# Three buffers for a batch's rows, transposes spread over two pairs, stacking in a new order, loads issued four and eight steps later

## The chip, the cores and the metric

One NeuronCore of a Trainium2 chip runs the whole program as one launch. The metric is the device time of one execution in microseconds; the time before is the median of three runs. TensorE is the matrix engine, VectorE, ScalarE and GpSimd are the three others, SyncE only issues transfers here; the profile writes them PE, DVE, ACT, POOL and SP.

## The reference

Attention with a threshold on the scores, for 8 batches of 8 heads, 576 tokens and 64 features a head, then a layer of 8 experts with one expert per token:

```python
scores = scale * np.matmul(q, k.transpose(0, 1, 3, 2))
thresh = np.max(scores, axis=-1, keepdims=True) - tau
scores = np.where(scores >= thresh, scores, -1000000000.0)
attn = np.exp(scores - np.max(scores, axis=-1, keepdims=True))
x = (attn / (attn.sum(-1, keepdims=True) + 1e-09)) @ v      # heads side by side: rows of 512
logits = x @ w_gate
expert_idx = np.argmax(logits, axis=1)
for e in range(E):                                        # 8 experts, 512 -> 1024 -> 512
    mask = expert_idx == e
    ye = np.maximum(x[mask] @ w1[e], 0.0) @ w2[e]
    out[mask] = gate_w[mask, None] * ye                   # gate_w: softmax weight of the chosen expert
```

## The kernel before

**Pairs and steps.** The attention part works on 32 pairs of heads, four to a batch, each in ten steps; step k belongs to pair k // 10. In one step PE computes one tile of transposed scores of that pair (`st_unit`: the `st` matmuls of L455 and L389, two products because queries and keys are held as a high and a low half in float16), ACT takes its exponential (L485 or L469), and DVE multiplies it with the mask "score not under the threshold" (L488, L470). In the same step PE computes one tile of plain scores of the pair two further on (`s_unit`: L405 and L408), and DVE reduces it to row maxima (L418). The maxima of a pair are turned by PE (`pst`, L429), split into three float16 rows (`ptT`) and sent by DMA into three extra rows of the buffer `CQ` of that pair, so that the next pair's `st` product already has the threshold subtracted. Between them stand the pieces of the product with the values of the pair before (`av_piece`, L534 to L546), nine to a pair, one to a step, from the step that `av` in the table `TUNE` names.

**What feeds a pair.** `load_qk` and `load_v` fetch queries, keys and values by DMAs issued from ACT's queue. `split` makes the high and low halves `hi` and `lo` (ACT L302 and L304, then POOL). `stack` copies them by twelve DMAs into the layout that PE wants: per head `QK` and `ck` (four DMAs, functions `first` and `low`) and the queries once more into `CQ` (`query`, two per head). All of these are issued from SP's queue, except that for the pairs 10, 14, 18, 22, 26 and 30 (`crowded`) the queries are issued from ACT's queue, two and three steps later. `split_v` casts the values to float16 in `vop`.

**Batch ends.** After each batch's last pair, `finish` normalizes its rows `R` (four tiles of 128 tokens, and a fifth half-tile `Rh` for every second batch) and SP issues one DMA transpose for each (`turn`, L627), 14 to 16 steps after; `logits`, `route`, `ranks` and the indirect sends (`send`, POOL L725) of the rows to the expert buffers in DRAM follow in the steps of the next pairs. `R` has two buffers; the numbers of the rows (`ids`, L688 and L690) are copied into them by ACT, which must wait until the sends of the batch before have read the buffer.

**What sets the order.** `plan` and `after(k, f, where)` put closures into numbered steps, in front, in the middle or at the end of one, and that order is each engine's program order, up to the end of the attention part (step 320, less 16). The experts after it are ordered by the framework's scheduler. Every engine works through its queue in order. The framework adds semaphore waits by itself; the DMAs of SP and ACT together take eight completion counters in turn, and a DMA waits until the one that had its counter before has landed.

Of the kernel before, what the change touches and what calls it, by code (L numbers as in the profile page):

```python
# [10 lines left out]
F16 = mybir.dt.float16  # L11
F32 = mybir.dt.float32
I32 = mybir.dt.int32
# [31 lines left out]
CAP = NTOK  # L45

TUNE = dict(
    lead=10, cast=1, sl=10, ll=15, sp0=6, sps=0, lv=-9, sv=-2, av=2, tr=4, d=2, lg=5, d5=2, d6=2, d7=1, lg7=9, km=16, rate=15, dh=1, do=3, w1d=5, plv=1, xv=3, so=0, sto=0, ord=0, sc=5, fa=3, fd=4, wa1=-70, wa2=-86, wl1=-28, wl2=-6, avb=2, route=1, ranks=7, pp=8, ew=4, maskat=0, w1a=-40, w1b=3,
)


# [1 line left out]
def kernel(  # L53
# [36 lines left out]

    NM = 3
    KC = 64 + NM
    NB = 3
    NQ = 4
    NV = NT
    cks = [[cpool.tile([P, S], F16, name=f"ck_{i}_{a}") for a in range(2)] for i in range(NQ)]
    cqs = [op.tile([P, 9 * P], F16, tag=f"CQ{i}", name=f"CQ_{i}", bufs=1) for i in range(NQ)]
    vops = [cpool.tile([P, NV, 2 * D + 1], F16, name=f"vop_{i}") for i in range(NB)]
    vfs = [cpool.tile([P, 10, D + 1], F32, name=f"vf_{i}") for i in range(NB)]

    def fill(i, eng):
        for a in range(2):
# [148 lines left out]
    def after(k, f, where=END):  # L251
        plan(now[0] + k, f, where)
# [54 lines left out]
    def stack(n):  # L307
        d = st[n]
        hi, lo = d["hi"], d["lo"]
        d["CK"] = cks[n % NQ]  # L310
        d["QA"], d["KB"] = [], []

        d["CQ"] = CQ = cqs[n % NQ]
        if n >= NQ:
            nc.gpsimd.memset(CQ[64:KC].bitcast(U32), 0)
        def first(a, QK, r):
            return [
                lambda e: e.dma_start(QK[0:64], hi[r]),
                lambda e: e.dma_start(QK[64:128, 1], hi[r, 1]),
            ]  # L320
# [12 lines left out]

        heads = []
        for a in range(2):
            QK = op.tile([P, 2, S], F16, tag=f"QK{a}", name=f"QK_{n}_{a}")
            heads.append((a, QK, slice(64 * a, 64 * a + 64)))
            d["QA"].append(QK[:, 0])
            d["KB"].append(QK[:, 1])
        x, y = heads  # L340
        if n == 1:
            for h, e in ((x, nc.sync), (y, nc.scalar)):
                for f in first(*h) + query(*h) + low(*h):
                    f(e)
            return
        if n == 2:
            for part in first, query, low:
                for h in heads:
                    for f in part(*h):
                        f(nc.sync)  # L350
            return
        for h in heads:
            (f0, f1), (l0, l1) = first(*h), low(*h)
            for f in f0, l0, f1, l1:
                f(nc.sync)
        crowded = n > 9 and n % 4 == 2
        for i, f in enumerate(f for h in heads for f in query(*h)):
            if crowded:
                after(2 + i // 2, lambda f=f: f(nc.scalar))
            else:  # L360
                f(nc.sync)

    def split_v(n):
        vop, x = vops[n % NB], vfs[n % NB][:, 0:NV, 0:D]
# [55 lines left out]
    def parts(n):  # L420


        nm = st[n]["nm"]
        r = small.tile([P, 9], F32, tag="r", name=f"r_{n}")
        nc.vector.tensor_reduce(r, nm.rearrange("p a t -> p t a"), axis=AX.X, op=ALU.min)

        def turn():
            ps = ps_m.tile([P, 512], F32, tag="m", name=f"pst_{n}")
            nc.tensor.transpose(ps[0:9, 0:P], r, ident)  # L429
            x, y = ps[0:9, 0:P], ps[0:9, P:2 * P]  # L430
            t = small.tile([9, 3, P], F16, tag="ptT", name=f"ptT_{n}", bufs=1)
            v, a = nc.vector, nc.scalar
            for i, f in enumerate((
                lambda: (a.activation(t[:, 0], x, AF.Identity, bias=thr[0:9]), n or rows(t, 0)),
                lambda: v.scalar_tensor_tensor(y, x, thr[0:9], t[:, 0], ALU.add, ALU.subtract),
                lambda: (a.copy(t[:, 1], y), n or rows(t, 1)),
                lambda: (v.tensor_tensor(t[:, 2], y, t[:, 1], ALU.subtract), rows(t, *(range(3) if n else (2,)))),
            )):
                after(i, f, MID)

        def rows(t, *ps):
            for p in ps:
                (nc.sync if n else nc.scalar).dma_start(
                    st[n]["CQ"][64 + p:65 + p].rearrange("p (t c) -> p t c", t=9), t[:, p]
                )

        after(3 if n else 1, turn, FRONT)

    def st_unit(n, t):
# [10 lines left out]
        if t in WHOLE:  # L460
            if t == CORNER:
                pf = pp.tile([P, w], F32, tag="pfc", name=f"e_{n}_{t}", bufs=2)
            elif "pe" in d:
                pf = d.pop("pe")[:, 1]
            else:
                d["pe"] = pp.tile([P, 2, 512], F32, tag="pf", name=f"e_{n}_{t}", bufs=5)
                pf = d["pe"][:, 0]
            d["Pf"][t] = pf
            nc.scalar.activation(pf, sc, AF.Exp, bias=ntau_f, scale=0.125 / SS)  # L469
            return lambda: nc.vector.scalar_tensor_tensor(pf, sc, 0.0, pf, ALU.is_ge, ALU.mult)  # L470
# [25 lines left out]
        return mask  # L496


    sent = set()
    sends = []  # L500
    SYNC = mybir.DependencyInfo(mybir.DependencyClass.Sync, mybir.DependencyReason.DATA)
    W = D + 1
    Rs = [rpool.tile([P, NT, ROW], I32, name=f"R_{i}") for i in range(2)]
    Rh = [rpool.tile([P, ROW], I32, name=f"Rh_{i}") for i in range(2)]
    xhs = [rpool.tile([P, H, W], F32, name=f"xh_{i}") for i in range(2)]

    def row(b, j):
        return Rs[b % 2][:, j] if j < NT else Rh[b // 2 % 2]

    def halves(x):  # L510
        return x.bitcast(F16).rearrange("p (c h d) -> p c h d", c=4, h=2)
# [76 lines left out]
            finish(b)  # L588

    def rounded(b, hp, x, js, eng):  # L590
        o = Rs[b % 2][:, js, 0:DM].bitcast(F16).rearrange("p j (c h d) -> p j c h d", c=4, h=2)[:, :, hp]
        x = x[:, js].rearrange("p j u d -> p j (u d)")

        def low():
            eng.tensor_tensor(o[:, :, 1], x, o[:, :, 0], ALU.subtract)

        def high():
            nc.scalar.copy(o[:, :, 0], x)
            after(1, low)

        after(int(eng is nc.gpsimd), high)

    def finish(b):
# [19 lines left out]
        def turn(j):  # L623
            if j % 2 == 0:
                xTs["t"] = rpool.tile([P, 2, 8, P], F16, tag="xT", name=f"xTg_{b}_{j}", bufs=3)
            xTs[j] = xT = xTs["t"][:, j % 2]
            nc.sync.dma_start_transpose(xT, row(b, j)[:, 0:DM].bitcast(F16))  # L627

        if n > NT:
            after(1 if last else 2, lone)  # L630
        t0 = 2 if last else 14 if b < B - 2 else 7
        for j in range(n):
            after(t0 + (j // 2 if t0 == 14 else j), lambda j=j: turn(j))
        d = t0 + ((n - 1) // 2 if t0 == 14 else n - 1)
# [24 lines left out]
    def route(b, n, dist, Lj, w, got):  # L659
# [25 lines left out]

        def ids(b, n):
            t = tid[:, b // 2]
            nc.scalar.copy(Rs[b % 2][:, :, DM + 1:DM + 2], t[:, 4 * (b % 2):4 * (b % 2) + NT].unsqueeze(2))  # L688
            if n > NT:
                nc.scalar.copy(row(b, NT)[:, DM + 1:DM + 2], t[:, 8:9])  # L690

        def gate(b, n):
            c = 1.0 / (SX * SW * SW)
            nc.scalar.activation(Rs[b % 2].bitcast(F32)[:, :, DM:DM + 1], sm[:, 0:NT], AF.Copy, scale=c)
            if n > NT:
                nc.scalar.activation(row(b, NT).bitcast(F32)[:, DM:DM + 1], sm[:, NT], AF.Copy, scale=c)

        def ranks():
# [239 lines left out]
    def fetch(m):  # L938
# [3 lines left out]
        if m in range(NF, NF + 2):  # L942

            Rm = row(B - 2, m - NF)
            at = 4 * ROW - (2 - (m - NF)) * DM
            xT = Rs[B % 2].rearrange("p j c -> p (j c)")[:, at:at + DM].bitcast(F16)
# [473 lines left out]
```

## Time and profile before

| what | before |
|---|---|
| median of 3 runs (977.92 to 983.87) | 979.29 us |
| the profiled execution | 990.7 us |
| its span, first to last instruction | 989.0 us |
| mean granted clock of TensorE | 0.972 |
| busy time of PE, DVE, ACT, POOL | 899.4, 643.1, 588.5, 496.5 us |
| the attention part within the span | to about 540 us |

The profile shows one execution. Its own time is 1.7 us above its span, and 11.4 us above the median of the runs. The granted clock is the share of TensorE's full speed (2.4 GHz) that the chip allowed in a stretch, so 0.50 is 1.2 GHz.

### The profile page before, as it was taken

How to read it: one execution, taken by the hardware profiler on the slowest of the kernel's cores; microseconds unless marked ns; L12 is line 12 of the kernel's file. 1: busy time of each engine (PE TensorE's matmuls, PEld its weight loads, DVE VectorE, ACT ScalarE, POOL GpSimd, SP SyncE). 2: the span in 40 equal slices, each digit the busy share in tenths (PEclk: the TensorE clock that was granted, in tenths of full speed). 3: DMA queues.
4: the chain of work that ended last, by engine and by line, in shares of the span. 5: the costliest groups of instructions: out<-in, count | busy, mean ns of one | idle time of the engine just before them, and what ended most of it. 6: DMA issues, size and time to landing. Idle time of an engine off the chain costs nothing. (4 is left out here: it accounts for less than half of the span.)

```text
span 989.0 us, 34524 instructions
## 1 busy us (share of the span) xinstructions
PE 899.4 (91%) x14655; PEld 647.8 (66%) x14655; DVE 643.1 (65%) x1322; ACT 588.5 (60%) x1042; POOL 496.5 (50%) x478
## 2 busy tenths in 40 slices
PE   4899988989989799899887797899999999999996
PEld 2477766757767577667665674777766677666773
DVE  7999969868878679697796845825342433424551
ACT  4799877958778587778665732524342433424551
POOL 7577756957858668578656422531222122212121
PEclk9999999989989999999998899999999999999999
DMA  7645575675845946646547549897556746558740
GB/s 190 157 120 142 120 150 125 160 136 140 180 100 137 182 107 167 148 111 163 111 108 143 152 152 314 246 257 233 174 156 165 243 113 207 159 153 189 233 145 25
DMA packets 178301, 158.55 MB, mean 160 GB/s; under 512 B 134557, under 2 KB 150431, under 8 KB 178144
## 3 DMA queue, kind: packets, MB, share of 16 engines
q1 hardware_dynamic: 123642, 98.86, 41.2%
q10 hardware_dynamic: 45510, 28.28, 10.9%
q0 software_dynamic: 8992, 29.18, 8.9%
q8 instruction: 116, 1.90, 0.8%
q14 instruction: 41, 0.34, 0.1%
HBM read 90.56 MB, written 19.17 MB: 111 GB/s over the span
## 5 line engine op out<-in xcount | busy, mean ns | idle before, releaser
L418 DVE TENSOR_REDUCE nm<-s 128x1 f32<-128x512 f32 (+1 forms) x320 | 200.3, 634 | 7.6 <-PE s L408 6.1
L389 PEld LDWEIGHTS <-wb 128*128 128x128 f16 x2304 | 186.9, 100 | 24.4 <-issue 5.1
L389 PE MATMUL y<-wb,hl 128*128 128x512 f16 (+2 forms) x1104 | 196.2, 347 | 0.0
L389 PE MATMUL h<-xTm,wb 128*128 128x256 f16 (+3 forms) x2112 | 191.6, 252 | 1.3 <-DVE e L470 0.7
L455 PE MATMUL st<-QK 128*64 128x64 f16 (+1 forms) x1152 | 147.2, 297 | 30.9 <-DVE e L488 20.2
L494 POOL TENSOR_TENSOR pl<-e,ph 128x1024 f16<-128x1024 f32 x63 | 135.0, 2144 | 78.8 <-ACT ph L493 70.4
L470 DVE SCALAR_TENSOR_TENSOR e<-st,e 128x512 f32<-128x512 f32 (+1 forms) x224 | 134.8, 614 | 49.5 <-ACT e L469 49.5
L405 PE MATMUL s<-QK 128*64 128x64 f16 (+1 forms) x1152 | 145.8, 296 | 20.8 <-POOL QK L135 8.2
L930 DVE SCALAR_TENSOR_TENSOR wb<-wf,wb 128x1024 f16<-128x1024 f32 x96 | 117.3, 1257 | 62.0 <-ACT wb L929 60.0
L389 PEld LDWEIGHTS <-hl 128*128 128x128 f16 (+2 forms) x1104 | 89.0, 98 | 97.6 <-issue 1.3
L408 PE MATMUL s<-ck,CQ 128*64 128x64 f16 (+1 forms) x1152 | 146.4, 294 | 1.5 <-DMA ck<-lo 1.5
L389 PE MATMUL st<-CQ,ck 128*64 128x64 f16 (+1 forms) x1152 | 142.2, 295 | 0.7 <-DMA CQ<-ptT 0.5
L469 ACT ACTIVATE e<-st,ntau_f 128x512 f32<-128x512 f32 (+1 forms) x224 | 133.5, 624 | 15.3 <-PE st L389 12.4
L485 ACT ACTIVATE e<-st,ntau 128x512 f32<-128x512 f32 x128 | 87.7, 685 | 58.7 <-PE st L389 24.5
L1068 POOL DMA_INDIRECT out_dram<-o,gt x39 | 43.2, 1107 | 156.1 <-ACT o L1065 144.9
L929 ACT ACTIVATE wb<-wf 128x1024 f16<-128x1024 f32 x96 | 97.5, 1050 | 35.2 <-DMA wf<-in_w_dram 15.5
L1016 ACT ACTIVATE hl<-h 128x512 f16<-128x512 f32 (+2 forms) x78 | 44.6, 572 | 120.1 <-PE h L389 102.5
L405 PEld LDWEIGHTS <-QK 128*64 128x64 f16 x1152 | 68.0, 115 | 61.4 <-issue 24.7
L488 DVE SCALAR_TENSOR_TENSOR e<-st,e 128x512 f32<-128x512 f32 x128 | 85.9, 672 | 24.9 <-ACT e L485 24.1
L455 PEld LDWEIGHTS <-QK 128*64 128x64 f16 x1152 | 64.9, 114 | 43.8 <-issue 35.2
L537 PE MATMUL av<-vf,e 128*64 128x65 f32 x2048 | 86.8, 225 | 0.7 <-issue 0.7
L537 PEld LDWEIGHTS av<-vf,e 128*64 128x64 f32 x2048 | 82.7, 142 | 1.2 <-issue 0.9
(228 smaller groups left out, 1453.0 us busy)
## 6 DMA issues: line engine op xcount, KB each, us to landing
wf<-in_w_dram SPq DMA_DIRECT2D x96, 512.0 KB
qkf<-in_qk_dram ACTq DMA_DIRECT2D x29, 576.0 KB
vf<-in_v_dram ACTq DMA_DIRECT2D x30, 320.0 KB
QK<-hi SPq DMA_DIRECT2D x61, 144.0 KB
QK<-hi SPq DMA_DIRECT2D x61, 72.0 KB
QK<-lo SPq DMA_DIRECT2D x61, 72.0 KB
ck<-lo SPq DMA_DIRECT2D x61, 72.0 KB
CQ<-hi SPq DMA_DIRECT2D x49, 64.0 KB
```

What stands on the lines that cost most here:

```text
L389: x = nc.tensor.matmul(*a, **kw).ins
L405: nc.tensor.matmul(sc[rows, oc], d["QA"][a][:, cols], d["KB"][a][:, CH[c]], start=True, stop=False)
L408: nc.tensor.matmul(sc[rows, oc], d["CQ"][:, at:at + cols.stop - cols.start], d["CK"][a][:, CH[c]], start=False, stop=True,)
L418: nc.vector.tensor_reduce(o, sc[:, 0:width(t)], axis=AX.X, op=ALU.max, negate=True)
L455: nc.tensor.matmul(sc[rows, oc], d["KB"][a][:, cols], d["QA"][a][:, CH[c]], start=True, stop=False)
L469: nc.scalar.activation(pf, sc, AF.Exp, bias=ntau_f, scale=0.125 / SS)
L470: return lambda: nc.vector.scalar_tensor_tensor(pf, sc, 0.0, pf, ALU.is_ge, ALU.mult)
L485: nc.scalar.activation(pf, sc, AF.Exp, bias=ntau, scale=0.125 / SS)
L494: (nc.vector if (n, t) in PLV else nc.gpsimd).tensor_tensor(l, pd, h, ALU.subtract)
L537: mm(av[rows, 1], pf[NT + j][:, q], vf[:, NT + j], start=False, stop=False)
L929: nc.scalar.activation(o[:, :, 0], x, AF.Copy, scale=SW)
L930: nc.vector.scalar_tensor_tensor(o[:, :, 1], x, SW, o[:, :, 0], ALU.mult, ALU.subtract)
```

## The change

A third buffer for the rows `R` (and one less for `vop`, `vf`, and one less of five for the float32 exponentials `pf`, to make room). The transposes of a batch's rows go to 16, 17, 18, 26 and 27 steps after its end instead of 14, 14, 15, 15, 16, and `logits` and all that follows it ten steps later; the last two batches stay as they were, and the sixth has its own list. The stacking of every pair is issued from SP, in the order `first`, `query`, `low`. `load_qk` moves from 5 to 9 within its pair's steps (`ll`), `load_v` from step 1 to step 9 (`lv`), `split_v` from step 8 of the pair before to step 4 (`sv`), `av` starts at step 1 instead of 2, and the three `rows` DMAs go out one step later. Before each indirect send POOL writes one element to a tile of its own (`apart`).

```diff
-    lead=10, ... ll=15, sp0=6, sps=0, lv=-9, sv=-2, av=2, ...
+    lead=10, ... ll=11, sp0=6, sps=0, lv=-1, sv=4, av=1, ...
...
-    NB = 3
+    NB = 2
...
-        for h in heads:
-            (f0, f1), (l0, l1) = first(*h), low(*h)
-            for f in f0, l0, f1, l1:
-                f(nc.sync)
-        crowded = n > 9 and n % 4 == 2
-        for i, f in enumerate(f for h in heads for f in query(*h)):
-            if crowded:
-                after(2 + i // 2, lambda f=f: f(nc.scalar))
-            else:
-                f(nc.sync)
+        for part in first, query, low:
+            for h in heads:
+                for f in part(*h):
+                    f(nc.sync)
...
-                lambda: (v.tensor_tensor(t[:, 2], y, t[:, 1], ALU.subtract), rows(t, *(range(3) if n else (2,)))),
+                lambda: (v.tensor_tensor(t[:, 2], y, t[:, 1], ALU.subtract), n or rows(t, 2)),
+                lambda: n and rows(t, *range(3)),
...
-                d["pe"] = pp.tile([P, 2, 512], F32, tag="pf", name=f"e_{n}_{t}", bufs=5)
+                d["pe"] = pp.tile([P, 2, 512], F32, tag="pf", name=f"e_{n}_{t}")
...
+    apart = small.tile([1, 1], F32, tag="apart", name="apart", bufs=1)
-    Rs = [rpool.tile([P, NT, ROW], I32, name=f"R_{i}") for i in range(2)]
+    NR = 3
+    Rs = [rpool.tile([P, NT, ROW], I32, name=f"R_{i}") for i in range(NR)]
...
-        t0 = 2 if last else 14 if b < B - 2 else 7
+        turns = {B - 1: range(2, 7), B - 2: range(7, 12), B - 3: (16, 16, 17, 17, 18)}.get(b, (16, 17, 18, 26, 27))
         for j in range(n):
-            after(t0 + (j // 2 if t0 == 14 else j), lambda j=j: turn(j))
-        d = t0 + ((n - 1) // 2 if t0 == 14 else n - 1)
+            after(turns[j], lambda j=j: turn(j))
+        d = turns[n - 1]
...
             def send(j):
+                nc.gpsimd.memset(apart, 0.0)
                 dma = nc.gpsimd.indirect_dma_start(
```

Three places of the program show the new order. In the rows below a name such as `CQ_2` is a buffer, `QK_10_0` the first head of pair 10, `e_7_2` the exponential of pair 7's tile 2.

SP's queue where the first batch's rows are transposed (pair 7), before and then after:

```order
119 L443 DMA CQ_3_107<-ptT_7_2889 1x9x128 x3
120 L627 DMA_TRANSPOSE xTg_0_0_3064<-R_0_197 128x8x128 x2
121 L627 DMA_TRANSPOSE xTg_0_2_3095<-R_0_197 128x8x128 x2
122 L318 DMA QK_10_0_3250<-hi_10_2976 64x1152
123 L324 DMA QK_10_0_3250<-lo_10_2977 64x576
124 L319 DMA QK_10_0_3250<-hi_10_2976 64x576
125 L325 DMA ck_2_0_100<-lo_10_2977 64x576
126 L318 DMA QK_10_1_3251<-hi_10_2976 64x1152
```

```order
119 L432 DMA CQ_3_107<-ptT_7_2890 1x9x128 x3
120 L618 DMA_TRANSPOSE xTg_0_0_3094<-R_0_196 128x8x128 x2
121 L618 DMA_TRANSPOSE xTg_0_2_3173<-R_0_196 128x8x128
122 L318 DMA QK_10_0_3266<-hi_10_2979 64x1152
123 L319 DMA QK_10_0_3266<-hi_10_2979 64x576
124 L318 DMA QK_10_1_3267<-hi_10_2979 64x1152
125 L319 DMA QK_10_1_3267<-hi_10_2979 64x576
126 L330 DMA CQ_2_106<-hi_10_2979 64x512
127 L331 DMA CQ_2_106<-hi_10_2979 64x64
128 L330 DMA CQ_2_106<-hi_10_2979 64x512
129 L331 DMA CQ_2_106<-hi_10_2979 64x64
130 L324 DMA QK_10_0_3266<-lo_10_2980 64x576
```

Four transposes stood in a row ahead of the stacking of pair 10; now three do, the fourth comes a pair later, and the queries (`CQ_2`) stand in SP's queue ahead of the `lo` halves.

ACT's queue in the same pair 7, before and then after:

```order
204 L434 ACTIVATE ptT_8_3304<-pst_8_3302,thr_155 9x128
205 L330 DMA CQ_2_106<-hi_10_2976 64x512
206 L331 DMA CQ_2_106<-hi_10_2976 64x64
207 L485 ACTIVATE e_7_2_3311<-st_7_3_3337,ntau_157 128x512
208 L330 DMA CQ_2_106<-hi_10_2976 64x512
209 L331 DMA CQ_2_106<-hi_10_2976 64x64
210 L493 CAST ph_7_0_3239<-e_7_0_3238 128x1024
```

```order
202 L422 ACTIVATE ptT_8_3308<-pst_8_3306,thr_153 9x128
203 L474 ACTIVATE e_7_2_3315<-st_7_3_3338,ntau_155 128x512
204 L482 CAST ph_7_0_3255<-e_7_0_3254 128x1024
205 L458 ACTIVATE e_7_8_3370<-st_7_8_3365,ntau_f_156 128x512
```

The four DMAs of the queries, between which an exponential stood, are gone from ACT.

ACT's queue in a pair without a batch end (pair 5), before and then after:

```order
157 L469 ACTIVATE e_5_8_2539<-st_5_8_2534,ntau_f_158 128x512
158 L469 ACTIVATE e_5_10_2546<-st_5_10_2541,ntau_f_158 128x64
159 L436 CAST ptT_6_2476<-pst_6_2474 9x128
160 L302 ACTIVATE qkf_9_2236<-qkf_9_2236 128x1152
161 L469 ACTIVATE e_5_8_2539<-st_5_9_2577,ntau_f_158 128x512
162 L288 DMA qkf_10_2649<-in_qk_dram 128x1152
163 L493 CAST ph_5_2_2484<-e_5_2_2483 128x1024
164 L304 CAST hi_9_2563<-qkf_9_2236 128x1152
165 L598 CAST R_0_197<-xn_3_2399 128x4x128
166 L469 ACTIVATE e_5_4_2671<-st_5_4_2666,ntau_f_158 128x512
```

```order
155 L458 ACTIVATE e_5_8_2539<-st_5_8_2534,ntau_f_156 128x512
156 L458 ACTIVATE e_5_10_2546<-st_5_10_2541,ntau_f_156 128x64
157 L424 CAST ptT_6_2477<-pst_6_2475 9x128
158 L353 ACTIVATE vop_1_109<-vf_1_111 128x4x64
159 L302 ACTIVATE qkf_9_2388<-qkf_9_2388 128x1152
160 L589 CAST R_0_196<-xn_3_2371 128x4x128
161 L458 ACTIVATE e_5_8_2539<-st_5_9_2580,ntau_f_156 128x512
162 L482 CAST ph_5_2_2485<-e_5_2_2484 128x1024
163 L304 CAST hi_9_2566<-qkf_9_2388 128x1152
164 L458 ACTIVATE e_5_4_2670<-st_5_4_2665,ntau_f_156 128x512
```

The cast of the values (`vop`) now stands ahead of the split of pair 9 (`qkf_9`), the cast of the rows `R` moved up behind it, and the load of `qkf_10` left this place.

## Rows read from the trace of the kernel before

**Rows 1.** The page, part 1: busy us, share of the span, instructions.

```profile
PE 899.4 (91%) x14655; PEld 647.8 (66%) x14655; DVE 643.1 (65%) x1322; ACT 588.5 (60%) x1042; POOL 496.5 (50%) x478
```

**Rows 2.** Waits of PE, 120 to 540 us: us in total, times, longest.

```profile
PE st L455 <- DVE e L488: 18.8, 6, 5.4
...
PE st L455 <- DVE e L470: 4.8, 9, 1.3
PE s L405 <- DVE e L470: 3.4, 3, 1.3
PE s L405 <- DVE nm L418: 2.9, 10, 0.3
PE pst L429 <- DVE row L748: 2.4, 1, 2.4
```

**Rows 3.** Waits of ACT, 120 to 540 us.

```profile
ACT e L485 <- DMA CQ<-hi: 16.8, 3, 5.9
...
ACT e L485 <- DMA QK<-hi: 7.5, 1, 7.5
ACT e L485 <- DMA QK<-lo: 5.2, 1, 5.2
ACT R L688 <- issue: 4.5, 1, 4.5
ACT Rh L690 <- DMA xs<-Rh,posi: 3.2, 1, 3.2
```

**Rows 4.** SP's timeline at the first batch end: start us, us, operation, count.

```profile
126.44 6.00 SPq L627 DMA_TRANSPOSE xTg<-R  x4
```

**Rows 5.** ACT's timeline there; brackets: idle before, and what ended it.

```profile
138.68 0.69 ACT L485 ACTIVATE e<-st,ntau 128x512 f32<-128x512 f32 x1 [5.18 <-DMA QK<-lo]
```

**Rows 6.** PE's timeline there.

```profile
140.14 0.22 PE L455 MATMUL st<-QK 128*64 128x64 f16 x2 [3.05 <-DVE e L488]
```

**Rows 7.** Windows: us, busy of PE, PEld, DVE, ACT, POOL; PEclk; DMA share; GB/s.

```profile
204.00:214.00 10.00, 6.46 (x132) 5.52 (x127) 4.41 (x9) 6.87 (x11) 3.70 (x2) 0.66 0.62 154
...
480.00:490.00 10.00, 6.97 (x173) 6.06 (x170) 4.36 (x10) 7.45 (x12) 4.29 (x3) 0.83 0.22 52
```

**Rows 8.** ACT's timeline, 102 to 120.5 us: a pair without a batch end.

```profile
105.33 0.69 ACT L485 ACTIVATE e<-st,ntau 128x512 f32<-128x512 f32 x1 [0.62 <-PE st L389]
...
111.95 2.03 ACT L469 ACTIVATE e<-st,ntau_f 128x512 f32<-128x512 f32 x3
113.88 0.41 ACT L365 ACTIVATE vop<-vf 128x256 f16<-128x256 f32 x1
...
119.77 0.69 ACT L485 ACTIVATE e<-st,ntau 128x512 f32<-128x512 f32 x1 [0.62 <-PE st L389]
```

**Rows 9.** DVE's timeline, 112 to 117 us.

```profile
112.66 0.69 DVE L470 SCALAR_TENSOR_TENSOR e<-st,e 128x512 f32<-128x512 f32 x1 [1.04 <-ACT e L469]
...
115.66 0.68 DVE L418 TENSOR_REDUCE nm<-s 128x1 f32<-128x512 f32 x1
```

**Rows 10.** PE's timeline, 110.8 to 119.2 us.

```profile
111.39 0.41 PE L455 MATMUL st<-QK 128*64 128x512 f16 x2
...
112.25 0.19 PE L542 MATMUL av<-vop,ph 128*64 128x64 f16 x1
...
112.63 0.41 PE L455 MATMUL st<-QK 128*64 128x512 f16 x2
...
116.79 0.41 PE L405 MATMUL s<-QK 128*64 128x512 f16 x2
...
117.55 0.41 PE L455 MATMUL st<-QK 128*64 128x512 f16 x2
...
119.13 0.38 PE L455 MATMUL st<-QK 128*64 128x512 f16 x2
```

**Rows 11.** DMA queues, 118 to 119.7 us (values): packets, MB, share of 16 engines.

```profile
q10 hardware_dynamic: 1283, 0.32, 85.1%
```

**Rows 12.** DMA queues, 123.4 to 126.4 us (queries and keys).

```profile
q10 hardware_dynamic: 143, 0.59, 59.9%
```

More of the change, by code (lines that the diff above doesn't have):

```diff
@@ L47 @@
 TUNE = dict(
-    lead=10, cast=1, sl=10, ll=15, sp0=6, sps=0, lv=-9, sv=-2, av=2, tr=4, d=2, lg=5, d5=2, d6=2, d7=1, lg7=9, km=16, rate=15, dh=1, do=3, w1d=5, plv=1, xv=3, so=0, sto=0, ord=0, sc=5, fa=3, fd=4, wa1=-70, wa2=-86, wl1=-28, wl2=-6, avb=2, route=1, ranks=7, pp=8, ew=4, maskat=0, w1a=-40, w1b=3,
+    lead=10, cast=1, sl=10, ll=11, sp0=6, sps=0, lv=-1, sv=4, av=1, tr=4, d=2, lg=5, d5=2, d6=2, d7=1, lg7=9, km=16, rate=15, dh=1, do=3, w1d=5, plv=1, xv=3, so=0, sto=0, ord=0, sc=5, fa=3, fd=4, wa1=-70, wa2=-86, wl1=-28, wl2=-6, avb=2, route=1, ranks=7, pp=8, ew=4, maskat=0, w1a=-40, w1b=3,
 )
@@ L92 @@
     KC = 64 + NM
-    NB = 3
+    NB = 2
     NQ = 4
     NV = NT
-    cks = [[cpool.tile([P, S], F16, name=f"ck_{i}_{a}") for a in range(2)] for i in range(NQ)]
+    cks = [[op.tile([P, S], F16, tag=f"ck{i}{a}", name=f"ck_{i}_{a}", bufs=1) for a in range(2)] for i in range(NQ)]
     cqs = [op.tile([P, 9 * P], F16, tag=f"CQ{i}", name=f"CQ_{i}", bufs=1) for i in range(NQ)]
-    vops = [cpool.tile([P, NV, 2 * D + 1], F16, name=f"vop_{i}") for i in range(NB)]
-    vfs = [cpool.tile([P, 10, D + 1], F32, name=f"vf_{i}") for i in range(NB)]
+    vops = [op.tile([P, NV, 2 * D + 1], F16, tag=f"vop{i}", name=f"vop_{i}", bufs=1) for i in range(NB)]
+    vfs = [op.tile([P, 10, D + 1], F32, tag=f"vf{i}", name=f"vf_{i}", bufs=1) for i in range(NB)]
     def fill(i, eng):
@@ L345, in stack @@
             return
-        if n == 2:
-            for part in first, query, low:
-                for h in heads:
-                    for f in part(*h):
-                        f(nc.sync)
-            return
-        for h in heads:
-            (f0, f1), (l0, l1) = first(*h), low(*h)
-            for f in f0, l0, f1, l1:
-                f(nc.sync)
-        crowded = n > 9 and n % 4 == 2
-        for i, f in enumerate(f for h in heads for f in query(*h)):
-            if crowded:
-                after(2 + i // 2, lambda f=f: f(nc.scalar))
-            else:
-                f(nc.sync)
+        for part in first, query, low:
+            for h in heads:
+                for f in part(*h):
+                    f(nc.sync)
     def split_v(n):
@@ L507, in row @@
     def row(b, j):
-        return Rs[b % 2][:, j] if j < NT else Rh[b // 2 % 2]
+        return Rs[b % NR][:, j] if j < NT else Rh[b // 2 % 2]
     def halves(x):
@@ L590, in rounded @@
     def rounded(b, hp, x, js, eng):
-        o = Rs[b % 2][:, js, 0:DM].bitcast(F16).rearrange("p j (c h d) -> p j c h d", c=4, h=2)[:, :, hp]
+        o = Rs[b % NR][:, js, 0:DM].bitcast(F16).rearrange("p j (c h d) -> p j c h d", c=4, h=2)[:, :, hp]
         x = x[:, js].rearrange("p j u d -> p j (u d)")
@@ L687, in ids @@
             t = tid[:, b // 2]
-            nc.scalar.copy(Rs[b % 2][:, :, DM + 1:DM + 2], t[:, 4 * (b % 2):4 * (b % 2) + NT].unsqueeze(2))
+            nc.scalar.copy(Rs[b % NR][:, :, DM + 1:DM + 2], t[:, 4 * (b % 2):4 * (b % 2) + NT].unsqueeze(2))
             if n > NT:
@@ L693, in gate @@
             c = 1.0 / (SX * SW * SW)
-            nc.scalar.activation(Rs[b % 2].bitcast(F32)[:, :, DM:DM + 1], sm[:, 0:NT], AF.Copy, scale=c)
+            nc.scalar.activation(Rs[b % NR].bitcast(F32)[:, :, DM:DM + 1], sm[:, 0:NT], AF.Copy, scale=c)
             if n > NT:
@@ L945, in fetch @@
             at = 4 * ROW - (2 - (m - NF)) * DM
-            xT = Rs[B % 2].rearrange("p j c -> p (j c)")[:, at:at + DM].bitcast(F16)
+            xT = Rs[(B - 2) % NR].rearrange("p j c -> p (j c)")[:, at:at + DM].bitcast(F16)
             xT = xT.rearrange("p (i c t) -> p i c t", i=1, c=8)
```

## Prediction

> **What bounds the kernel now.** I read the busy shares first: PE is busy 91% of the span, the others 50 to 65% [rows 1]. So an edit pays only where PE stands still or runs at a low clock. The attention part has both. In PE's waits the largest line is one of six: the first product of a new pair's scores waits 18.8 us in all for DVE's mask L488 [rows 2]. DVE is not the cause. ACT, which makes the exponential that this mask reads, waits at the same places for transfers: 16.8 us in three waits, 7.5 and 5.2 in one each [rows 3]; the sixth is smaller. The timelines of the first batch end show the chain. SP issues the four transposes of the batch's rows from 126.44 for 6.00 us [rows 4]; an exponential on ACT starts at 138.68 after 5.18 us of idle time, put down to stacking DMAs [rows 5]; PE resumes at 140.14 after 3.05 [rows 6]. In ACT's program the operation just ahead of that exponential is a pair of query DMAs for a crowded pair. An exponential doesn't need those; ACT stands at them, because each takes a completion counter that a transpose or a stacking DMA from SP still holds. Every one of the six batch ends with a crowded stack has this.
>
> A second loss follows it. In the windows behind the second to fourth of these ends (three alike, one shown) the granted clock is 0.66 over 10 us, so 3.4 us are lost in each; behind the sixth it is 0.83, 1.7 us [rows 7]. Ahead of each PE had stood for 3.0 to 5.4 us. Behind the first and fifth the clock stays full. The sum of the clock's loss is 3 x 3.4 + 1.7 = 11.9 us.
>
> Between batch ends the loop is tight, and that matters for the rest. In a pair without a batch end ACT waits for PE once (0.62 us at 105.33, again at 119.77: the period is 14.44 us) and then works through without a gap to the three exponentials at 111.95 [rows 8]. DVE waits for these, 1.04 us, until 112.66, and then works without a gap until the reduction at 115.66, which ends at 116.34 [rows 9]. PE starts the plain scores at 116.79, which need the bank that this reduction frees [rows 10]: 0.45 us to spare. From there PE reaches the product on which ACT waits at 119.77. Each lap is a chain ACT, DVE, PE, ACT of 14.44 - 0.45 = 13.99 us, while PE's own work is 14.44: PE bounds, by half a microsecond.
>
> **The change, part by part.**
>
> *Queries leave ACT's queue, one of the transposes leaves its neighbours.* The DMAs on which ACT stands at six batch ends are gone. The exponential behind them needs only PE's scores, so ACT's 5 us go, and PE's 18.8 with them. If PE no longer stands, I expect the clock to hold too: up to 18.8 + 11.9 = 30.7 us; if the clock still falls, 18.8. The nearest rows for what is left are ACT's stacking waits themselves: the loads of queries and keys in ACT's queue take counters too, but the DMAs that had them are now issued a whole pair earlier, or are rows. I take -28, leaving some 3 us for a stall that is not wholly gone. Late next at a batch end is the stacking on SP: its issue now stands behind three transposes, not four, and the queries add four issues ahead of the low halves; the pair that needs them begins its plain scores ten steps later, a period of 14.44 us, against some 6 us of transposes and as much of stacking. I take nothing for it.
>
> One rule speaks against this part. The Trainium skill, "DMA: Bandwidth & Descriptors", section "Rules for kernel authors", says that spreading DMAs over issuing engines gives no bandwidth and only saves issue time. By that alone, moving four issues from ACT to SP would be worth no more than ACT's issue slots, and the sum would lack its -28: 979.3 - 3 + 20 = 996. The trace shows 5 us of idle ACT there, which the rule doesn't speak of.
>
> *Three buffers for R.* The copy of row numbers into R or Rh waits for the sends of the batch before, 3.2 and 4.5 us among others [rows 3]. Behind the first two of three such copies PE waits four times 1.3 for the masks L470, 5.0 in all, and behind the last 2.4 at `pst` [rows 2]. With a third buffer the last is free of the sends, and the first meets sends that are further done; the middle one still waits. The gain is between 0 and 5 us; I take -3.
>
> *av one step earlier.* PE has the same products in a lap, in another place. A piece of the first kind makes a step of 119.13 - 117.55 = 1.58 us, one of the second kind of 112.63 - 111.39 = 1.24, of which 112.63 - 112.25 = 0.38 is the piece itself [rows 10]. Between the product that ACT waits for and the plain scores at 116.79 there is now one piece less, of the first kind: 0.38 + (1.58 - 1.24) = 0.72 us. It stands behind those scores instead. PE comes 0.72 us earlier to a bank that is not free earlier, and has 0.72 more to do before it serves ACT again.
>
> *split_v five steps later.* The cast of the values (0.41 us alone, some 0.31 in a packed run, since a neighbour begins before it ends) stood behind the three exponentials [rows 8]; now it stands ahead of them, in the run of ACT without a gap that DVE waits for. So DVE's reduction ends at 116.34 + 0.31 = 116.65, some 0.05 goes into the handover, and PE wants the bank at 116.79 - 0.72 = 116.07. PE waits 116.65 + 0.05 - 116.07 = 0.63 us in each lap, and the lap grows to 14.44 + 0.6 = 15.05. Bounds: if ACT's order hides the cast, 0.32; in laps where PE already waits for that reduction (rows with 2.9 us in ten waits [rows 2]) there was nothing to spare and it costs 0.31 + 0.72 = 1.03. Some 27 of the 32 laps lie in the steady loop: 8.6 to 27.8 us. A moving copy of R, which comes ahead of these exponentials too, was ahead of them before and costs nothing new. I take 0.75 a lap, a little above the quiet lap since some laps have nothing to spare: +20.
>
> *Loads at step 9.* In the trace the values keep the 16 DMA engines 85.1% busy for 1.7 us, so 1.45 us alone [rows 11]; queries and keys 59.9% of 3 us, 1.8 us [rows 12]. They are now issued together at step 9, and the split that reads the second stands at step 4 of the next pair, five steps of 1.44 us later: 7.2 us. Alone they need 3.3 us; sharing the engines evenly with the stacking, twice that, 6.6. Just in time: I take 0 and keep the case as a rival. The bound on the other side is no gain: among ACT's largest waits there is none for these loads [rows 3].
>
> *The rest.* 36 one-element writes on POOL, off the path (POOL is busy 50% [rows 1]); the smallest write on POOL in this trace takes 0.1 us, 3.6 in all, covered by POOL's idle time; if that were gone, 3.6 us. Four buffers of exponentials in place of five: the piece that frees each comes one step earlier, so the tile is free as early as before. Two buffers for the values: the load into one comes after the last piece that reads it. The transposes at step 26 and 27 delay `logits` and the sends by ten steps; for the first five batches nothing reads the sent rows before the attention part is over. The experts' part is ordered anew by the scheduler behind it: nothing in it is removed, and I give it 0, with 5 us on either side.
>
> The sum is -28 - 3 + 20 = -11 us: 990.7 - 11 = 979.7 in a profiled execution. The one shown lies 11.4 us above the median of the runs, so the forecast stands against the median: 979.3 - 11 = **968 us**.
>
> **The rivals.**
>
> *B, the loop takes it for free.* ACT absorbs the cast and PE its piece, 0 to 0.3 us a lap (0 to 8 us). For it: only one lap's spare time was read closely, and 0.45 us is little to argue from. Against: PE's waits for that reduction exist already in ten laps. 979.3 - 31 + 0 to 8 gives 948 to 956.
>
> *C, ending slower: the loads at step 9 land too late.* Both loads, near 3.3 us of all engines, now meet the twelve stacking DMAs of step 0, and the split of the keys stands in ACT's run ahead of the exponentials. If the second load lands at the split or up to 1 us after it, ACT waits up to 1 us in each lap, on top of the loop's 0.75: 27 x 0.5 to 1.0 = +14 to +27, so 982 to 995. It decides from 27 x 0.4 = 11 us on: there the gain is used up. For it: the margin of 7.2 against 6.6 us is thin. Against: SP's stacking moves little data beside them. The Trainium skill, "DMA: Bandwidth & Descriptors", section "Queues, rings and completion order", says that each DMA engine takes packets in turn from the queues with work, which is what sharing evenly means; no row here separates it from first come, first served, by which the loads would be done in 3.3 us and this rival would fall.
>
> *D, the batch ends stay.* The eight counters are shared by ACT and SP, and ACT still issues two loads in each lap; if one meets a counter held by a transpose, ACT stands as before, with the cost of the loop on top: 979.3 + 6 to 20, so 985 to 1000. Against: in the new program the loads come ahead of the transposes of their step.
>
> **How the numbers follow.** The forecast has a chance of 0.50 (955 to 978 by the bounds of the loop, 8.6 and 27.8, and the batch ends' 18.8 to 30.7), B 0.22, C 0.18, D 0.10. A change within 1% (969.5 to 989.1) is about what a measurement of this kernel can't tell from none. Of the forecast's 0.50 some 0.27 lies under 969.5; with all of B that is 0.49 faster. The rest of the forecast and half of C and D make 0.34 within, and 0.17 is slower. The range must hold 8 in 10: from 950, which leaves out the best of B, to 988, which leaves out the worse part of C and most of D.
>
> **What would show it.** Right: no exponential of ACT waits for a stacking DMA at the six batch ends, the 18.8 us of PE's line are under 3, and the clock is 1.00 in the four windows; against that PE's waits on the reduction L418 or the mask ahead of it have grown from 2.9 us to 15 or more, and the lap of the sample pair is near 15 us. Wrong: a lap still at 14.4 (B), ACT waiting at the split for the load in every pair (C), or 5 us waits of ACT at batch ends, at another line (D). The clock could also fall in the laps where PE waits 0.6 us, which would cost more than any of these terms.

## The result, and the profile after

The changed kernel takes 0.9918 of the time before (95% interval 0.9890 to 0.9946, 20 runs of each), some 8 us less. That ratio leaves out slow runs, five of the changed kernel's 20 and one of the other's; the medians of all 20 are 976.5 and 981.4 us, 4.9 us apart. The forecast was 968 with a range of 950 to 988; its working said -11 us. The profiled execution of the changed kernel took 977.9 us.

Page, part 1, after (to be set beside [rows 1]):

```profile
PE 897.6 (92%) x14655; PEld 641.1 (66%) x14655; DVE 638.9 (65%) x1322; ACT 583.1 (60%) x1042; POOL 497.4 (51%) x508
```

Work per engine is as before; what moved is where PE stands. Waits of PE in the changed kernel, 120 to 540 us (us in total, times, longest), beside [rows 2]:

```profile
PE st L377 <- DMA CQ<-ptT: 10.6, 3, 5.5
PE s L393 <- issue: 7.1, 3, 5.8
PE st L444 <- DVE e L459: 5.7, 12, 1.0
PE s L393 <- DVE nm L406: 3.5, 6, 1.8
PE s L393 <- DVE e L459: 3.4, 2, 1.8
PE av L528 <- DVE e L459: 2.5, 6, 1.5
```

The line of 18.8 us in six waits is gone from the list. One line is new: waits for the rows of the maxima (`CQ<-ptT`), 10.6 us in three. Another grew from 0.9 to 7.1 us, 5.8 of them in one wait that the profile puts down to nothing ("issue"). The waits for DVE's masks and reductions add up to 5.7 + 3.5 + 3.4 + 2.5 = 15.1 us, but lines of these kinds in [rows 2] made 4.8 + 3.4 + 2.9 = 11.1 before. ACT, beside [rows 3]:

```profile
ACT R L679 <- DMA xs<-R,posi: 14.1, 2, 10.6
```

No exponential waits for a stacking DMA any more. The copy of row numbers waits 14.1 us in two places instead of 3 to 5 us in three. The four windows of which [rows 7] shows two, and one more behind the first batch end:

```profile
204.00:214.00 10.00, 10.00 (x241) 7.77 (x238) 9.44 (x21) 8.12 (x16) 8.11 (x10) 1.00 0.95 256
272.00:282.00 10.00, 9.87 (x261) 7.86 (x258) 8.75 (x19) 8.38 (x14) 9.18 (x12) 1.00 0.90 257
341.00:351.00 10.00, 6.67 (x187) 4.72 (x180) 7.12 (x14) 6.73 (x10) 8.19 (x7) 1.00 0.53 135
480.00:490.00 10.00, 7.37 (x143) 5.41 (x145) 2.90 (x6) 6.08 (x12) 1.49 (x1) 0.67 0.64 124
148.00:158.00 10.00, 4.53 (x54) 2.70 (x48) 4.59 (x10) 2.17 (x6) 3.10 (x4) 0.83 1.06 138
```

Three clocks rose from 0.66 to 1.00. The fourth window fell from 0.83 to 0.67, and 148 to 158 us is new. The low clock moved more than it went; these windows stand around the other new waits:

```profile
234.00:244.00 10.00, 7.35 (x101) 5.03 (x99) 6.95 (x19) 3.84 (x12) 2.76 (x3) 0.83 0.66 168
348.00:358.00 10.00, 7.53 (x105) 5.25 (x103) 5.64 (x11) 3.80 (x10) 3.49 (x3) 0.83 0.86 200
474.00:494.00 20.00, 12.45 (x274) 8.67 (x270) 7.34 (x19) 9.41 (x20) 7.95 (x6) 0.74 0.82 128
```

With 148 to 158 us that is 3 x 1.7 and some 5 us, 10 us lost to the clock in all, against 11.9 before. What stalled PE in the window from 148 us and in the last one stands in two rows of PE and one of ACT:

```profile
153.92 0.64 PE L377 MATMUL st<-CQ,ck 128*64 128x512 f16 x2 [5.47 <-DMA CQ<-ptT]
...
480.99 0.26 PE L393 MATMUL s<-QK 128*64 128x64 f16 x1 [5.83 <-issue]
```

```profile
483.92 0.20 ACT L679 COPY R<-tid 128x4 int32<-128x4 int32 x1 [10.60 <-DMA xs<-R,posi]
```

At 153.92, one pair after the first batch end, PE waits for the maxima rows of the pair. SP's timeline shows how late they went out:

```profile
144.88 0.59 SPq L325 DMA_DIRECT2D ck<-lo  x1
145.57 2.46 SPq L432 DMA_DIRECT2D CQ<-ptT  x3
148.08 1.27 SPq L618 DMA_TRANSPOSE xTg<-R  x1
```

They stand behind the stacking, which itself began late behind three transposes, and the loads of values, queries and keys are issued around 147 to 148 us, with the fourth transpose. In pair 27 ACT stands 10.6 us at the row numbers of the last batch, until the last send from that buffer, issued at 470.81, has landed. These copies are emitted behind the part with the order by hand, so the scheduler put them far ahead into ACT's queue; the sends of the batch that has the buffer now run ten steps later.

The quiet lap can be read from an operation that ACT does once in each pair (in the kernel before it starts at 107.66 and 122.10):

```profile
110.59 0.24 ACT L424 CAST ptT<-pst 9x128 f16<-9x128 f32 x1
125.59 0.24 ACT L424 CAST ptT<-pst 9x128 f16<-9x128 f32 x1
```

15.00 us where 14.44 was. And PE waits where the chain said, though for the mask of one step, not for the reduction beside it, and the profile shows only 0.19 of the 0.56 us as idle time:

```profile
116.64 0.41 PE L444 MATMUL st<-QK 128*64 128x512 f16 x2 [0.19 <-DVE e L459]
```

A surprise is where this one execution gained. The first product of pair 30 starts at the same time in both:

```profile
526.81 0.41 PE L455 MATMUL st<-QK 128*64 128x512 f16 x2
```

(before), and after:

```profile
526.93 0.38 PE L444 MATMUL st<-QK 128*64 128x512 f16 x2
```

With spans of 989.0 and 976.1, the stretch behind it took 462.2 and 449.2 us: in this pair of executions, 13 us apart, the whole gain lies there, while in the attention part the batch ends' gain was spent again.

### The profile page after: what moved, and what is told of

Read it like the earlier page. It is cut to its first block, busy times and chain, and to the rows that moved or that the text cites. A ratio compares the mean times of both kernels' runs of the same rounds, so it can differ in the third digit from the quotient of the medians.

```text
span 976.1 us, 34419 instructions
## 1 busy us (share of the span) xinstructions
PE 897.6 (92%) x14655; PEld 641.1 (66%) x14655; DVE 638.9 (65%) x1322; ACT 583.1 (60%) x1042; POOL 497.4 (51%) x508
## 5 line engine op out<-in xcount | busy, mean ns | idle before, releaser
L377 PEld LDWEIGHTS <-wb 128*128 128x128 f16 x2304 | 183.1, 98 | 23.7 <-issue 6.2
L444 PE MATMUL st<-QK 128*64 128x64 f16 (+1 forms) x1152 | 144.9, 296 | 13.0 <-DVE e L459 12.0
L922 DVE SCALAR_TENSOR_TENSOR wb<-wf,wb 128x1024 f16<-128x1024 f32 x96 | 114.4, 1230 | 54.2 <-ACT wb L921 54.0
L377 PE MATMUL st<-CQ,ck 128*64 128x64 f16 (+1 forms) x1152 | 139.3, 292 | 10.6 <-DMA CQ<-ptT 10.6
L1060 POOL DMA_INDIRECT out_dram<-o,gt x39 | 45.6, 1170 | 130.3 <-ACT o L1057 117.9
L393 PEld LDWEIGHTS <-QK 128*64 128x64 f16 x1152 | 66.8, 114 | 68.7 <-issue 35.4
L528 PE MATMUL av<-vf,e 128*64 128x65 f32 x2048 | 85.9, 223 | 2.5 <-DVE e L459 2.5
L477 DVE SCALAR_TENSOR_TENSOR e<-st,e 128x512 f32<-128x512 f32 x128 | 85.4, 669 | 3.3 <-ACT rs L545 2.1
L444 PEld LDWEIGHTS <-QK 128*64 128x64 f16 x1152 | 63.8, 112 | 35.3 <-issue 23.3
```

The costliest lines, as they stand in the source:

```text
L377: x = nc.tensor.matmul(*a, **kw).ins
L393: nc.tensor.matmul(sc[rows, oc], d["QA"][a][:, cols], d["KB"][a][:, CH[c]], start=True, stop=False)
L444: nc.tensor.matmul(sc[rows, oc], d["KB"][a][:, cols], d["QA"][a][:, CH[c]], start=True, stop=False)
L528: mm(av[rows, 1], pf[NT + j][:, q], vf[:, NT + j], start=False, stop=False)
L922: nc.vector.scalar_tensor_tensor(o[:, :, 1], x, SW, o[:, :, 0], ALU.mult, ALU.subtract)
```

## Experiments

Twelve kernels, each against the kernel before on its own chip. The theory under test has three parts: the queries in ACT's queue are what stalls the batch ends; the laps of 15.0 us come from `av` and `sv` together, by one chain with 0.45 us to spare; the new stalls come from the loads and from the copies of row numbers. The rivals are in the expectations.

**The chain.** The kernel before with `av=1` alone:

```diff
- ... sv=-2, av=2, ...
+ ... sv=-2, av=1, ...
```

> The kernel before with av=1 alone: the pieces of the value product one step earlier, nothing else. Chain theory (each lap is a chain ACT, DVE, PE, ACT with 0.45 us to spare): the quiet lap grows from 14.44 by 0.72 - 0.45 = 0.27 to about 14.7 us, +6 to +8 us in all. Rival (the laps of 15.0 us in the changed kernel come from its loads and stacking, not from these two edits): the lap stays at 14.4, and the time within 3 us of before. The six batch ends keep their stalls by both.

With `sv=4` alone:

```diff
- ... sv=-2, av=2, ...
+ ... sv=4, av=2, ...
...
 def send(j):
+    nc.gpsimd.memset(apart, 0.0)
```

> The kernel before with sv=4 alone (the cast of the values ahead of ACT's three exponentials) and the one-element write ahead of each send, without which this order can't be built. Chain theory: 0.36 us more in the chain against 0.45 to spare, so the quiet lap stays at 14.4 to 14.5 us and the time within 4 us of before. A theory in which each edit costs by itself: lap 14.75, +8 us. It also prices the one-element writes: 0 by the prediction.

With both (and the same write in `send`):

```diff
- ... sv=-2, av=2, ...
+ ... sv=4, av=1, ...
```

> The kernel before with av=1 and sv=4 (and the one-element writes). Chain theory: the two are not additive, since 0.45 us is to spare once: lap 14.44 + 0.72 + 0.36 - 0.45 = 15.05 us, as in the changed kernel, and +16 to +22 us in all. Rival (loads and stacking make the long laps): lap 14.4 to 14.6, time within 5 us of before.

The lap of pairs 5 to 6, from ACT's rows in the kernel with av=1:

```profile
108.72 0.24 ACT L436 CAST ptT<-pst 9x128 f16<-9x128 f32 x1
123.41 0.24 ACT L436 CAST ptT<-pst 9x128 f16<-9x128 f32 x1
```

with sv=4:

```profile
108.09 0.24 ACT L436 CAST ptT<-pst 9x128 f16<-9x128 f32 x1
122.64 0.24 ACT L436 CAST ptT<-pst 9x128 f16<-9x128 f32 x1
```

and with both:

```profile
111.64 0.24 ACT L436 CAST ptT<-pst 9x128 f16<-9x128 f32 x1
126.64 0.24 ACT L436 CAST ptT<-pst 9x128 f16<-9x128 f32 x1
```

So 14.69, 14.55 and 15.00 us, against 14.7, 14.4 to 14.5 and 15.05 expected. The sum of the two single losses, 0.25 + 0.11 = 0.36, is less than the 0.56 of both: in this lap the spare time was spent once, as in the chain. The whole times are 1.0165 (1.0127 to 1.0203), 1.0083 (1.0059 to 1.0107) and 1.0216 (1.0167 to 1.0266). Both together cost 2.2%, 21 us, within the 16 to 22 expected; each alone costs more than its quiet lap says (16 and 8 us, expected 6 to 8 and under 4), so the laps near batch ends lose more than the quiet ones. In these profiles only four laps in a row, ahead of the first batch end, are this short, and as whole times the single costs add up to 24 us, no less than both: that the spare time is spent once shows in the quiet lap alone. With av=1 PE also waits for the rows of the maxima, which has no line in the kernel before:

```profile
PE st L389 <- DMA CQ<-ptT: 10.0, 6, 3.1
```

With both edits it is 9.6 us in five. The rival, that loads and stacking make the long quiet laps, falls. The one-element writes weren't run by themselves; they are inside the 0.8%.

**The queries.** The kernel before, all queries from SP, old order:

```diff
- crowded = n > 9 and n % 4 == 2
+ crowded = False
```

> The kernel before with the queries of the crowded pairs issued from SP like all others (old order, transposes as before, four and five in a row). If ACT's place in the queue of counters is the cause of the batch-end stalls: ACT's waits of 5 us at the six ends go, PE's 18.8 us fall under 4, the clock holds there, and the time is 20 to 30 us below before. If the transposes in a row are the cause whatever queue the queries are in: the stalls stay as waits for stacking or maxima rows, the time is within 5 us of before, and only their spreading helps.

0.9779 (0.9741 to 0.9817), 21 us less. Waits of PE, 120 to 520 us (pair 30 starts 19 us earlier here): of the 18.8 us for L488 0.6 is left, but L470, the mask of the tiles behind it, grew from 4.8 to 11.7:

```profile
PE st L455 <- DVE e L470: 11.7, 9, 3.0
...
PE st L455 <- DVE e L488: 0.6, 1, 0.6
```

and in ACT three waits remain, at its next DMA, the load of queries and keys (the operation behind it is named):

```profile
ACT ph L493 <- DMA QK<-hi: 10.2, 3, 4.6
```

The transposes stood in a row as before, so their row alone is not what stalls PE; ACT's DMAs are. Two of the six batch ends still stall PE, by 2.7 and 2.8 us, behind the loads in ACT's queue: the mechanism of rival D. The third wait of PE of that size, 3.0 us, which the expectations below count with them, is at no batch end; it ends at 489.6 us, in pair 28, behind a wait of ACT for expert weights.

The same with the whole new stacking, highs, queries, lows:

```diff
- for h in heads:
-     (f0, f1), (l0, l1) = first(*h), low(*h)
-     for f in f0, l0, f1, l1: f(nc.sync)
- ... queries
+ for part in first, query, low:
+     for h in heads:
+         for f in part(*h): f(nc.sync)
```

> The kernel before with the changed kernel's stacking alone: all from SP, highs first, queries, lows last. The queries on SP in the old order gave 0.978. If the order of remainders matters: 3 to 8 us below that, 0.970 to 0.975, or as much above it. If only the queue matters: 0.975 to 0.981, and the three waits of PE of 2.7 to 3.0 us that were left at batch ends stay.

0.9701 (0.9658 to 0.9743), 29 us less: the fastest kernel of this study, and by these ratios faster than the changed kernel by 2%. Its largest waits of PE in the same stretch:

```profile
PE st L443 <- DVE e L458: 6.4, 8, 2.3
PE pst L417 <- DVE run L670: 6.0, 5, 1.5
PE st L443 <- DVE e L476: 5.2, 2, 2.6
```

ACT's waits at its own loads fell from 10.2 us in three to 6.0 in two:

```profile
ACT ph L481 <- DMA CQ<-hi: 6.0, 2, 4.2
```

Up to pair 30 its clock falls in two places:

```profile
205.00:215.00 10.00, 7.12 (x121) 4.30 (x117) 6.84 (x19) 7.80 (x18) 7.65 (x6) 0.83 0.61 144
438.00:448.00 10.00, 7.37 (x172) 6.21 (x169) 5.46 (x11) 8.01 (x14) 6.96 (x6) 0.83 0.52 135
```

That is 2 x 1.7 = 3.4 us in place of 11.9. Its quiet lap is that of the kernel before. So the order of the remainders looks worth 0.8% on top of the queue; the two intervals just overlap at 0.974.

**The parts of the changed kernel, undone.** The cast of the values behind the exponentials again:

```diff
- ... sv=4, av=1, ...
+ ... sv=8, av=1, ...
```

> The changed kernel with sv=8: the cast of the values behind ACT's three exponentials again. Chain theory: the quiet lap falls from 15.00 to 14.7 us (only the piece of av is left in the chain), some 20 to 27 laps, -6 to -8 us against the changed kernel, so about 0.985 of before. Rival (the lap is held by loads and stacking at step 9 and 0): it stays at 15.0 and the time at 0.99.

0.985 (0.9749 to 0.995), as expected, with a wide interval; the lap is sharper:

```profile
108.62 0.24 ACT L424 CAST ptT<-pst 9x128 f16<-9x128 f32 x1
123.31 0.24 ACT L424 CAST ptT<-pst 9x128 f16<-9x128 f32 x1
```

14.69 us, where the loads and the stacking were those of the changed kernel.

The copies of row numbers at a step by hand:

```diff
 def finish(b):
+    if b in (B - 3, B - 2):
+        after(2, lambda: ids(b + 1, NT + (b + 1) % 2))
...
- lambda: ids(b, n),
+ *([lambda: ids(b, n)] if b < B - 2 else []),
```

> The changed kernel with the row numbers of the last two batches copied at a step put by hand (two steps after the end of the batch before), when the sends that read the buffer are over; in the changed kernel the scheduler puts these copies earlier into ACT's queue, where ACT stands 3.5 and 10.6 us. If that wait is on the path: ACT's two waits go, PE's idle 5.8 us and the half clock behind it (10.2 us at half speed) in pair 27 too, -8 to -12 us, about 0.98 of before. If PE's idle time there has another cause: within 2 us of the changed kernel.

0.9907 (0.988 to 0.9935), not below the changed kernel's 0.9918 by any amount that can be told. ACT's two waits are gone, and so is PE's 5.8 us with the half clock in pair 27:

```profile
462.00:483.00 21.00, 17.61 (x406) 13.14 (x402) 17.01 (x40) 14.36 (x31) 16.34 (x15) 0.99 0.83 179
```

The clock there is 0.99. That the time doesn't follow is a miss. Part of it is size: in three variants that kept the copies where they were (with sv=8, with the loads apart, with the transposes in a row) ACT's two waits took 11.3, 8.9 and 6.0 us instead of 14.1, so the one profiled execution showed a large case. And the profiled execution of this variant, 964.8 us, was the fastest of its ten; PE waits 11.8 us in five for the maxima rows in it. Where the rest went stays open.

The loads apart and earlier:

```diff
- ... ll=11, ... lv=-1, ...
+ ... ll=15, ... lv=-4, ...
```

> The changed kernel with the loads apart and earlier (ll=15 as before, lv=-4: queries and keys at step 5, values at step 6). The changed kernel waits 5.5, 2.7 and 2.5 us for the rows of the maxima (CQ<-ptT) one pair after three batch ends, where both loads, the fourth transpose and late stacking meet. If the loads at step 9 hold those rows: the three waits fall under 1 us each, with their half-clock stretches -10 to -15 us, about 0.98 of before. If the transpose and the late stacking hold them: the waits stay above 2 us and the time within 4 us of the changed kernel.

0.9937 (0.9903 to 0.9972). The waits for the maxima rows fell, but others came:

```profile
PE st L444 <- DVE e L459: 16.0, 15, 6.7
PE st L444 <- DVE e L477: 6.7, 2, 3.6
PE st L377 <- DMA CQ<-ptT: 6.0, 6, 2.0
```

From 5.5 us at the longest to 2.0 (1 was expected), so the loads at step 9 make the long ones; the shorter ones come with av=1 alone too, up to 3.1 us. But L477, the batch-end line that had vanished, is back. The loads trade one stall for another, and the time stays: neither expectation is met in full.

The transposes in a row again:

```diff
- .get(b, (16, 17, 18, 26, 27))
+ .get(b, (16, 16, 17, 17, 18))
```

> The changed kernel with the transposes of every batch in a row again (steps 16, 16, 17, 17, 18), logits and sends eight to nine steps earlier with them. If spreading carries the gain at the batch ends: PE waits 3 to 5 us again at six batch ends, +10 to +25 us. If the queries on SP carry it: batch ends lose 1 to 3 us for a longer row of transposes, the waits for maxima rows a pair later (10.6 us) and the 10.6 us wait of ACT in pair 27 go, and the time is 5 to 15 us below the changed kernel.

0.9967 (0.9924 to 1.001): some 5 us worse than the changed kernel, with intervals that overlap, where I expected 5 to 15 us better. The wait for maxima rows didn't go, it became longer:

```profile
PE st L377 <- DMA CQ<-ptT: 14.1, 3, 6.7
```

So spreading the transposes is worth a little at most, not the batch ends' gain; and a fourth transpose a pair later is not needed to make those rows late.

The same with two row buffers:

```diff
- NR = 3
+ NR = 2
```

> The changed kernel with the transposes in a row (as in the run before) and two row buffers in place of three. The profiles of the changed kernel and its variants need 428 to 433 us from the start of the last pair to the end, those of the kernel before and its variants 439 to 444. If the third buffer is what shortens that last stretch: it grows to 438 to 444 here, and the time is 1.00 to 1.01 of before. If it is the loads, the stacking or the order that the scheduler found: it stays at 428 to 433 and the time at 0.997.

Its four runs lie between 968.6 and 996.3 us and settle no time. Its profile answers the question: pair 30 starts at 531.67, the span is 980.1, so the stretch behind it took 448.4 us, as in the changed kernel. The third buffer is not what shortens it.

```profile
531.67 0.38 PE L444 MATMUL st<-QK 128*64 128x512 f16 x2
```

**A version made of the parts that looked good.** The queries on SP in the old order, and the load of queries and keys at step 9:

```diff
- crowded = n > 9 and n % 4 == 2
+ crowded = False
...
- ... ll=15, ...
+ ... ll=11, ...
```

> The kernel before with the queries on SP and the load of queries and keys at step 9 (ll=11), as in the changed kernel. With the queries on SP alone, three batch ends kept a wait of PE of 2.7 to 3.0 us, behind ACT, which stands 10.2 us in three waits at its own load of queries and keys while SP's stacking holds its counter. If that is so, the load at step 9 clears them: 8.5 us and the half clock behind them (three stretches of 3.4 us, 5 us), so 0.965 to 0.97 of before. If another wait takes their place, or the load comes too late for the split: 0.978 or above.

1.006 (1.0037 to 1.0082): 2.9% above the same kernel with ll=15, where 1% less was expected. PE waits for the maxima rows (120 to 540 us; 0.4 us with ll=15), and ACT stands in quiet laps too (60 to 520 us):

```profile
PE st L389 <- DMA CQ<-ptT: 12.7, 5, 5.8
```

```profile
ACT rs L554 <- DMA QK<-lo: 22.8, 11, 2.7
```

ACT's operation named is the one behind the load of the values. In its row, and in SP's ahead of it:

```profile
93.14 0.21 ACT L554 ACTIVATE rs<-y 128x8 f32<-128x8 f32 x1 [1.26 <-DMA QK<-lo]
```

```profile
85.83 0.53 SPq L318 DMA_DIRECT2D QK<-hi  x1
89.34 0.51 SPq L324 DMA_DIRECT2D QK<-lo  x1
```

By the waits in the two programs, with ll=15 the load of the values takes the counter that the first stacking DMA had (`QK<-hi`), with ll=11 that of the second, `QK<-lo`. That one SP issues 3.5 us later, since it waits for POOL's remainders. A load that nobody had moved now waits in eleven laps, and in six more for another DMA that had its counter (6.9 and 6.0 us). How the 2.9% divides between these waits and those for the maxima rows isn't shown.

That with the row numbers by hand:

```diff
+ after(18 if b == B - 3 else 12, lambda: ids(b + 1, ...))
```

> The same with the row numbers of the last two batches copied at a step put by hand, behind the sends that read their buffers. The kernel before waits 3.2, 3.1 and 4.5 us in ACT for these copies, and PE some 5 to 7 us behind them. If those are on the path: 3 to 7 us below the run with the load at step 9, 0.960 to 0.966 of before. If not: the same as it.

1.0034 (1.0011 to 1.0058): 2.6 us below the run above, about what was expected of the copies at the least, with intervals that overlap; the kernel it builds on had already lost the gain.

## Why the prediction was right, and where not

**Batch ends, -28: right for the edit alone.** The new stacking alone gave -29 us (0.9701), and the stall was where the prediction had put it, in ACT's queue; there the clock came back with it, 3.4 us lost up to pair 30 in place of 11.9. In the changed kernel the 18.8 us went too, but new stalls brought their own low clock, and 10 us were lost to it. The Trainium skill, "DMA: Bandwidth & Descriptors", section "Rules for kernel authors", says that another issuing engine only saves issue time. The runs show 0.9779 for that move alone, so here it was worth more: an engine that computes stood in front of its DMA until an earlier one had landed.

**The loop, +20: right in size, its lap shown.** 15.00 us a lap (15.05 predicted) in the changed kernel and in the kernel before with the two edits, and +21 us of time. But the prediction spread its lap over 27 laps in a steady loop, and with both edits alone only four are quiet. Most of the 21 us came in laps that hold work of a batch end, where waits that it had not listed have a part (9.6 us for maxima rows); that the average comes near its 0.75 a lap is partly luck. Nor did its sign appear as stated: it compared 15 us of waits for masks and reductions with 2.9 for the reductions alone, and against 11.1 for both kinds they grew by 4.

**The sum: near by luck.** From the first product of pair 4 to that of pair 30 the profiled executions took 440.5 us before (86.3 to 526.8), 412.8 with the new stacking alone (85.9 to 498.7), 461.6 with the two loop edits (89.1 to 550.7) and 438.9 in the changed kernel (88.0 to 526.9). So -27.7 and +21.1 leave -6.6, if they add up, which no run shows; -1.6 was measured. Some 5 us went into stalls that the prediction put at nothing, and the gain of the profiled pair came from behind pair 30, where it had 0. The time is near the forecast by terms that cancel, not by terms that are small:

**Three buffers, -3: wrong in sign in the profile.** The step that failed is "the last is free of the sends". The first copy (`Rh`) waits no more and the middle one still waits, 3.5 us, both as forecast; the last waits 10.6. With three buffers it follows the sends of batch 4, which moved ten steps later; the scheduler put it in pair 27, not 30; and the last of these sends took 13 us to land (the median of the DMAs on `xs` is 4.7). PE stood 5.8 us, and the clock in the window from 480 us lost 3.3. Without the copies' waits the time was the same within 0.4%, so what it cost on average is less than this execution shows.

**Loads at step 9, 0: mis-sized.** In the changed kernel's profile the margin against the split held: ACT never waits there. It was thin, as rival C said: in three variants with the same loads ACT waits at the split (3.1 us with sv=8, 4.1 with the transposes in a row, 8.4 with two row buffers). And PE waited 10.6 us in three places for maxima rows, sent beside these loads and behind late stacking. Rival C had named the collision and put its victim wrong. Moving the loads away again gave nothing in the changed kernel, and in the kernel before, with the queries on SP, the one load at step 9 cost 2.9%, with waits for maxima rows and at the counters.

**The rest, 0: wrong.** From pair 30 to the end the changed kernel needed 449.2 us against 462.2. In the profiles of its five variants that stretch is 447 to 453, in those of the kernel before and its seven variants 455 to 462 (each the span less the start of pair 30's first product). So it is no accident of one execution. It is not `av` or `sv` (460 us with both), not the queue of the queries (458), not the third buffer (448 without it), not the transposes (451). The order of the stacking can have half of it at most (455). What is left is the later load of the values with its two buffers, four buffers of exponentials, maxima rows one step later, and the order that the scheduler found for the rest. There is one edit more that the diff above leaves out: the buffers `ck`, `vop` and `vf` moved from a pool that lasts to the end into the attention part's pool, which is closed before the weights of all experts but the first are loaded. None was run by itself, and it stays open.

**The rivals.** B fell with the lap of 15.00. D's mechanism exists (ACT at its loads, 10.2 us with the queries on SP in the old order), and the new order of stacking lessens it (6.0 us). The change of some 8 us lies 3 above the forecast's -11, the median of 976.5 us inside the range; it is within 1%, a band that the prediction gave 0.34. Two of its sums don't come out: 0.23 of the forecast and half of C and D make 0.37 within 1% and leave 0.14 slower, not 0.34 and 0.17; and by both bounds at once the forecast's upper end is 985 us, not 978. Its list of PE's waits left out the second line, 7.5 us in six at `pst` behind DVE's L682: that is 1.6 in the changed kernel and 2.0 with av=1 alone, a gain for which it has no term.

## What to carry to other kernels

Before moving work, write down the chain of one lap with the time to spare in each link; here 0.45 us was to spare, two edits wanted 0.72 and 0.36 of it, and together they cost 2.2%. Where completion counters are shared in turn, look for each DMA in a computing engine's queue at the DMA that had its counter before, and at when that one is issued; adding, removing or moving one DMA can change this for the others, as moving one load by four steps did here. Test a bundle's parts alone: one of these edits gave -3% and two others took most of it back.

## What the runs showed that I had not expected

A load that was not moved began to wait 1.3 to 2.7 us in eleven laps, 22.8 us in all, because another load's place among the DMAs had changed. And a stall of PE was not always followed by a low clock. In the kernel before PE stood 3.05 us until 140.14 [rows 6], and the clock stayed full:

```profile
138.00:148.00 10.00, 7.61 (x212) 5.90 (x212) 5.56 (x12) 8.65 (x15) 5.49 (x3) 1.00 0.45 120
```

Behind 3.03 us, until 483.40, the window from 480 us had 0.83, and behind 3.54, until 207.65, the one from 204 us had 0.66 [rows 7].
